# Pooled attention and a routed expert layer: VectorE's score differences first, banks by longest free, preparation at other steps

## The chip, the core and the metric

The program runs on one core of a Trainium2 chip. The metric is the device time of one execution in microseconds (us). A core has TensorE (PE; its weight loads are listed apart as PEld), VectorE (DVE), ScalarE (ACT), GpSimd (POOL) and SyncE (SP), which here issues the transfers between HBM and the on-chip memory SBUF. TensorE writes its results to PSUM, a small memory of banks that VectorE and ScalarE read. Each engine runs its instructions in order.

## What is computed

```python
# q, k, v: 8 batches, 8 heads, 1152 rows, 64 columns
q_pool = q.reshape(B, H, S // 2, 2, D).mean(axis=3)          # 576 pooled queries
scores = scale * np.matmul(q_pool, k.transpose(0, 1, 3, 2))
scores = scores - np.max(scores, axis=-1, keepdims=True)
attn = np.exp(scores)
attn = attn / (np.sum(attn, axis=-1, keepdims=True) + 1e-09)
x = np.matmul(attn, v)                                        # to 4608 tokens x 512
# expert layer: 8 experts, 512 -> 1024 -> 512
logits = x @ w_gate
e_idx = np.argmax(logits, axis=1)                             # one expert per token
gate_w = softmax(logits)[token, e_idx]
eom = 1.0 / (1.0 + np.exp(-(x @ w_output_gate)))
out = gate_w * eom[e_idx] * (np.maximum(x @ w1[e_idx], 0.0) @ w2[e_idx])
```

## The kernel before

Values are kept as a high and a low part (for instance `xk` and `kp` of k, `ph` and `pl` of the exponentials), and products are sums of two or three matmuls, so that the result has nearly 32-bit precision.

**Order.** Attention works on 32 pairs of heads (8 batches, 4 pairs each). A pair takes 18 steps: two heads, nine key blocks of 128 each. The main loop goes over the steps s of all pairs and writes out by hand the order of the instructions of TensorE, VectorE, ScalarE and GpSimd. The order of SP's transfers, and the place of the expert stage's first weight splits, are left to a planner that goes by its own costs. In the prediction "phase p" is step p of a pair. A step of the kernel before does, in this order:

1. `pendv`: the pending differences of the step before (below).
2. `pop()`: one entry of the list `fill` of small VectorE operations.
3. `scores` (L288, L290): four matmuls into one of two score buffers `sps`; then ScalarE takes the exponential twice. In twelve of the 18 steps GpSimd forms the low part `pl` (L304). In the six of `PLP` = 1, 3, 7, 9, 13, 15 (nine in the last pair) ScalarE writes the second exponential back to the score buffer (L294, L295), and VectorE forms `pl` from it (L298, the function `lo`), queued in `pendv` for the next step.
4. the row maxima that a later pair needs, one or two chunks: a group of matmuls L241 into a bank `mp`, and a VectorE maximum over it (L242), with a `pop()` after each. They run up to 18 steps ahead. After 15 and 27 chunks `rows` transposes the maxima on TensorE (L268) into a bank, and VectorE splits them into a high and a low part (L271, L272), which SP copies into rows 66 and 67 of `qb`.
5. P times V (`av`, L317 to L319) for the pair's probabilities, in bursts six or more steps later. After a head's ninth block two entries go to the head of `fill`: `e01` (L326, L327: the reciprocal of the row sum) and `e2` (L330: the scaling of the output into `xb`).
6. `routers`: the gate logits of a finished pair (`logits`: transposes L374, copies L378 on ScalarE, differences L381, matmuls L389, L393 on VectorE), every other step, at the end of odd steps; with a batch's last pair, `router` goes on with some 20 small VectorE operations (L418 to L478), a few per step, and five scatters on GpSimd. The router of the sixth batch is followed by `setup`, which picks the expert that comes first (L651 to L659 and on).

At three places within a step, `prep_at` issues the preparation of pairs to come, by the table `PREP`: each entry has a time in thirds of a step. `lk`, `lv` load q, k, v; `kh`, `qh` (ScalarE) and `kl`, `qsum`, `ql`, `qd` (GpSimd) split them; `dk`, `dq`, `dl` copy the parts on SP's queue; `amax` (ScalarE, L180) takes absolute sums of V; `gmax` (TensorE, L184) sums them over the partitions; `scale` turns this into a power of two on VectorE, GpSimd and VectorE; `vh` (ScalarE), `vs` and `vl` (GpSimd) scale and split V.

**Banks.** The chunk maxima, the transposes, the logits, `gmax` and the router share three PSUM banks. `psum()` hands them out in rotation and skips the ones in the set `ring[1]`, which only the router's two long-lived tiles enter. A new tile in a bank waits for the readers of the bank's previous tile.

After the attention, the expert stage gathers tokens in tiles of 256 and runs the two layers of their expert.

Of the kernel before, what the change touches and what calls it, by code (L numbers as in the profile page):

```python
# [8 lines left out]
F32 = mybir.dt.float32  # L9
# [6 lines left out]
ALU = mybir.AluOpType  # L16
# [4 lines left out]
L0 = 15.5  # L21
LS = 0.037
RI = 7
PREP = ((0, 'lk'), (12, 'kh', 0), (13, 'kh', 1), (12, 'qsum'), (15, 'kl'), (18, 'dk', 0), (19, 'dk', 1), (21, 'qh'), (26, 'ql'), (26, 'dq', 0), (27, 'dq', 1), (29, 'qd'), (32, 'dl', 0), (33, 'dl', 1),
        (53, 'lv'), (71, 'amax', 0), (74, 'amax', 1), (81, 'gmax'), (82, 'scale', 0), (85, 'scale', 1), (90, 'scale', 2), (93, 'vh', 0), (93, 'vs', 0), (96, 'vh', 1), (97, 'vl', 0), (100, 'vs', 1), (104, 'vl', 1))
BURST = {0: 2, 2: 2, 4: 2, 6: 2, 8: 1, 10: 2, 12: 2, 14: 2, 16: 3}
PLP = (1, 3, 7, 9, 13, 15)
PLPL = (1, 3, 5, 7, 9, 11, 13, 15, 17)
# [31 lines left out]
def attention(tc, qT, kT, vL, wg, keep, xrows, idscr, cum, pairs, setup, scat, init):  # L60
    nc = tc.nc
    nb = len(pairs) // 4
    with ExitStack() as ctx:
# [14 lines left out]
        ring = [0, set()]  # L78

        def psum(hold=False, name="tp"):  # L80

            ring[0] = next(i % 3 for i in range(ring[0] + 1, ring[0] + 4) if i % 3 not in ring[1])
            if hold:
                ring[1].add(ring[0])
            x = ps_m.tile([128, 512], F32, name=name, tag=f"mp{ring[0]}")
            return (x, ring[0]) if hold else x

        ident = keep['ident']
        onesf = keep['onesf']
# [22 lines left out]
        def prep(n, table):  # L112
# [67 lines left out]
                nc.scalar.activation(out=j, in_=vp[:, NC * h:NC * h + NC], func=AF.Abs, scale=2.0 ** -17, accum_out=am[:, h:h + 1])  # L180

            def gmax():
                g = psum()[:, 0:2]
                nc.tensor.matmul(g, lhsT=onesf, rhs=am, start=True, stop=True)  # L184
                gm.append(g)

            def scale(i):
                if i == 0:
                    nc.vector.tensor_scalar(out=ex, in0=gm[0].bitcast(U32), scalar1=0x7F800000, scalar2=None, op0=ALU.bitwise_and)
                elif i == 1:  # L190
# [69 lines left out]
                k -= 1  # L260

        pend_t = []

        def rows(force=False):
            while pend_t and (force or now[0] >= pend_t[0][-1] + TLAG):
                m9, nt, t0, t1, qbf, _ = pend_t.pop(0)
                tp = psum()[0:nt, 0:128]
                nc.tensor.transpose(out=tp, in_=m9[:, 0:nt], identity=ident)  # L268
                mr = sm.tile([5, 2, 128], F32R, name="mr")[0:nt]
                c0 = 16.0 * SHIFT  # L270
                nc.vector.tensor_scalar(out=mr[:, 0], in0=tp, scalar1=c0, scalar2=None, op0=ALU.subtract)  # L271
                nc.vector.scalar_tensor_tensor(out=mr[:, 1], in0=tp, scalar=c0, in1=mr.bitcast(F32)[:, 0], op0=ALU.subtract, op1=ALU.subtract)  # L272
                for j in range(2):
                    dmaf(qbf[66 + j:67 + j, 128 * t0:128 * t1].rearrange("o (t n) -> o t n", n=128), mr[:, j])

        pendv = []

        def scores(st, h):
            ka, kb, qa, qb = st['ka'], st['kb'], st['qa'], st['qb']
# [27 lines left out]
        def av(st, h, xb):  # L307
            vt = st['vt']
            a = ps_a.tile([128, 512], F32, name=f"av{st['n']}", tag="av")
            av_ = a[:, 0:325].rearrange("p (b x) -> p b x", x=65)  # L310
            pop(99)
            for c in range(NC):
                ph, pl = st['ph', h, c], st['pl', h, c]
                for qb in range(5):
                    q0 = 128 * qb if qb < 4 else NQ - 128
                    hi, lo = ph[:, q0:q0 + 128], pl[:, q0:q0 + 128]
                    nc.tensor.matmul(av_[:, qb, 0:65], lhsT=hi, rhs=vt[:, h, c, 0:65], start=c == 0 and qb == 0, stop=False)  # L317
                    nc.tensor.matmul(av_[:, qb, 0:64], lhsT=hi, rhs=vt[:, h, c, 66:130], start=False, stop=False)  # L318
                    nc.tensor.matmul(av_[:, qb, 0:65], lhsT=lo, rhs=vt[:, h, c, 0:65], start=False, stop=c == NC - 1 and qb == 4)  # L319
# [5 lines left out]
            def e01():  # L325
# [3 lines left out]
            def e2():  # L329
# [35 lines left out]
        def logits(b, c, xb):  # L365
# [2 lines left out]
            xl = sm.tile([128, NQ], F32R, name="xl", bufs=1)  # L368
            yield 1
            for c0, c1, grp in ((0, 256, (0, 1)), (256, NQ, (2, 3, 4))):  # L370
                tx = psum()
                for i, t in enumerate(grp):
                    x = xb[:, t, 128 * c:128 * c + 128]
                    nc.tensor.transpose(out=tx[:, 128 * i:128 * i + 128], in_=x, identity=ident)  # L374
                d = 0
                for o, w in ((0, c1 - c0),) if c0 == 0 else ((0, 256), (320, 64)):
                    z = slice(c0 + d, c0 + d + w)
                    nc.scalar.copy(out=xh[:, z], in_=tx[:, o:o + w])  # L378

                    def sub(o=o, w=w, z=z, tx=tx):  # L380
                        nc.vector.tensor_tensor(out=xl[:, z], in0=tx[:, o:o + w], in1=xh.bitcast(F32)[:, z], op=ALU.subtract)  # L381
                    fill.insert(0, sub)
                    d += w
                yield 1
# [15 lines left out]
        def router(b, xb):  # L400
# [40 lines left out]
            ring[1].discard(tk)  # L441
            yield 1
            rk, rkk = psum(True)
            rv = cut(rk, 0, 5, 8)
# [31 lines left out]
            cs = cut(rk, 96, 8)  # L476
            V.tensor_reduce(out=cs, in_=ohb.rearrange("p t e -> p e t"), axis=AX.X, op=ALU.add)
            V.tensor_tensor(out=cum, in0=cs, in1=cum, op=ALU.add)  # L478
            ring[1].discard(rkk)
            for t in range(5):  # L480
                for _ in range(3):
                    yield
# [6 lines left out]
                if t == 2 and b < nb - 1:  # L489
                    wr()  # L490
            if b == max(nb - 3, 0):
                yield from setup(psum)

        def sgen():
            for n in range(len(pairs)):
# [24 lines left out]
        def prep_at(s, ph):  # L520
            u = 3 * (s + SLEAD) + ph
            for n in range(max(u // 54 - 2, 0), min(u // 54 + 2, NP)):
                r = u - 54 * n + min(3 * (LEAD - 15), 2 * n)
                if r == 0:
                    preps[n] = prep(n, PREP)
                if n in preps:
                    for f in preps[n].pop(r, ()):
                        f()

        E = mybir.EngineType  # L530
        with tc.manual_schedule(engines={E.PE, E.DVE, E.Activation, E.Pool}):
# [15 lines left out]
            for s in range(18 * NP + 14):  # L547
# [52 lines left out]
class Moe:  # L600
# [35 lines left out]
    def setup(self, psum):  # L636

        nc, kp, k, P1 = self.tc.nc, self.kp, self.keep, self.P1
        V = nc.vector
# [5 lines left out]
        V.tensor_copy(out=cb, in_=self.cum)  # L645
        yield
        yield 1
        cp = psum()
        nc.tensor.matmul(cp[:, 0:8], lhsT=k['ones'], rhs=cb, start=True, stop=True)
        cn = kp.tile([128, 8], F32, name="cn1")  # L650
        V.tensor_copy(out=cn, in_=cp[:, 0:8])  # L651
        yield
        mx = kp.tile([128, 1], F32, name="mx1")
        em = k['em8'][:, 0]
        V.tensor_reduce(out=mx, in_=cn, axis=AX.X, op=ALU.max)
        V.tensor_tensor(out=cn, in0=cn, in1=mx.broadcast_to([128, 8]), op=ALU.is_equal)
        yield
        V.tensor_tensor(out=cn, in0=cn, in1=em, op=ALU.mult)
        V.tensor_reduce(out=mx, in_=cn, axis=AX.X, op=ALU.min)  # L659
        yield  # L660
        V.tensor_scalar(out=k['ef'][:, 1:2], in0=mx, scalar1=8.0, scalar2=None, op0=ALU.add)
        V.tensor_tensor(out=k['oh1'], in0=em, in1=mx.broadcast_to([128, 8]), op=ALU.is_equal)
        V.memset(k['ef'][:, 0:1], 0.0)
        yield
        V.tensor_copy(out=k['es'], in_=k['ef'][:, 1:2])
        ri = kp.tile([128, 2], U32, name="ri1")
        rb = kp.tile([128, 1], F32, name="rb1")
        V.tensor_scalar(out=rb, in0=k['ef'][:, 1:2], scalar1=float(ESTRIDE), scalar2=None, op0=ALU.mult)
        V.tensor_tensor(out=ri, in0=k['Tp'][:, 0], in1=rb.broadcast_to([128, 2]), op=ALU.add)
        yield  # L670
        self.gather_ids(-1, ri, kp, 1)
        for _ in range(8):
# [325 lines left out]
```

## Time and profile before

| | |
|---|---|
| median of 3 runs | 1615.24 us (1612.62 to 1616.14) |
| the profiled execution | 1615.64 us, span 1613.5 us |
| busy: PE, PEld | 1531.1 us (95%), 1415.6 us (88%) |
| busy: DVE, ACT, POOL | 1083.9, 1077.8, 997.9 us |
| granted TensorE clock, mean | 0.986 |
| attention, first to last score matmul | 34 to 1066 us |

In a row of a timeline the columns are start and duration in us, engine, line, operation, the tiles written and read, shapes, and how many equal instructions the row joins; in brackets stands how long the engine was idle before and what ended it. In a row of waits the columns are who waited for whom, us in total, times, and the longest. Matmuls are pipelined: a row's duration is its latency, and the distance of two starts is what one costs. Weight loads overlap the matmuls before them.

### The profile page before, as it was taken

The page shows a single profiled execution, that of the slowest core. Times are in us where ns is not written, and L with a number is a line of the kernel's source. Part 1 is how long each engine was busy: PE and PEld are TensorE (multiplying, and loading weights), DVE is VectorE, ACT ScalarE, POOL GpSimd, SP SyncE. Part 2 cuts the span into 40 slices and gives each one's busy share as a digit, 9 for nine tenths or more (in the row PEclk, how much of TensorE's full clock was granted, in tenths as well). Part 3 has the DMA queues.
Part 4 walks back from the last instruction along what each step waited for, and adds up shares of the span by engine and source line. Part 5 has one row for each costly group of instructions (what it writes and reads, how often), then busy time and mean ns, then how long its engine had stood idle before and what let it go on. Part 6 is the DMA issues. An engine that isn't in the chain of part 4 may idle for free. (4 is left out here: it accounts for less than half of the span.)

```text
span 1613.5 us, 42264 instructions
## 1 busy us (share of the span) xinstructions
PE 1531.1 (95%) x16618; PEld 1415.6 (88%) x16618; DVE 1083.9 (67%) x2222; ACT 1077.8 (67%) x1862; POOL 997.9 (62%) x917
## 2 busy tenths in 40 slices
PE   4999999999999999999999999979999999999997
PEld 4998989989989989988998898868999999999996
DVE  4676776777677677776777777656666666656663
ACT  2887878877878888888878787754445444544441
POOL 4887888788879788879788878634332232233200
PEclk9999999999999999999999999979999999999999
DMA  7765455655556467547655565256455645363500
GB/s 207 219 156 145 132 155 144 161 141 142 152 153 157 126 150 188 135 116 183 152 141 142 150 162 132 74 183 224 157 176 178 204 166 197 105 217 112 203 22 25
DMA packets 88755, 245.49 MB, mean 152 GB/s; under 512 B 13082, under 2 KB 17370, under 8 KB 88546
## 3 DMA queue, kind: packets, MB, share of 16 engines
q1 hardware_dynamic: 78826, 221.07, 49.1%
q0 software_dynamic: 9728, 21.67, 4.3%
q8 instruction: 135, 2.21, 0.6%
q14 instruction: 66, 0.54, 0.1%
HBM read 165.04 MB, written 23.81 MB: 117 GB/s over the span
## 5 line engine op out<-in xcount | busy, mean ns | idle before, releaser
L242 DVE TENSOR_REDUCE pm<-mp 128x1 f32<-128x384 f32 x864 | 457.6, 551 | 232.0 <-PE mp L241 226.3
L304 POOL TENSOR_TENSOR pl<-p,ph 128x576 f16<-128x576 f32 x381 | 489.3, 1286 | 182.1 <-ACT ph L303 146.0
L241 PE MATMUL mp<-ka,qa 128*128 128x384 f32 x960 | 319.7, 349 | 21.0 <-DMA qa<-yq 18.6
L302 ACT ACTIVATE p<-sps 128x576 f32<-128x576 f32 x381 | 250.8, 658 | 115.3 <-PE sps L290 108.4
L288 PE MATMUL sps<-qa,ka 128*128 128x288 f32 x1152 | 280.3, 325 | 24.1 <-DVE pl L298 17.8
L317 PEld LDWEIGHTS <-ph 128*128 128x128 f16 x2880 | 261.8, 97 | 42.2 <-issue 29.5
L317 PE MATMUL av<-vt,ph 128*128 128x65 f16 x2880 | 295.7, 194 | 0.0
L318 PE MATMUL av<-vt,ph 128*128 128x64 f16 x2880 | 293.3, 194 | 0.0
L319 PE MATMUL av<-vt,pl 128*128 128x65 f16 x2880 | 292.4, 192 | 0.0
L318 PEld LDWEIGHTS <-ph 128*128 128x128 f16 x2880 | 265.4, 97 | 0.4
L319 PEld LDWEIGHTS <-pl 128*128 128x128 f16 x2880 | 265.7, 99 | 0.0
L241 PE MATMUL mp<-kb,qb 66*128 66x384 f32 x768 | 263.4, 343 | 0.6 <-DMA kb<-kp 0.6
L290 PE MATMUL sps<-qb,kb 68*128 68x288 f32 x1152 | 248.8, 298 | 2.0 <-DMA qb<-mr 2.0
L303 ACT ACTIVATE ph<-sps 128x576 f16<-128x576 f32 x381 | 249.4, 655 | 0.0
L288 PEld LDWEIGHTS sps<-qa,ka 128*128 128x128 f32 x1152 | 184.3, 192 | 36.6 <-PE av L319 22.3
L241 PEld LDWEIGHTS mp<-ka,qa 128*128 128x128 f32 x960 | 181.3, 193 | 24.3 <-issue 20.6
L772 PE MATMUL hps<-xh,w1h 128*128 128x256 f32 x704 | 200.4, 285 | 0.0
L772 PE MATMUL hps<-xl,w1h 128*128 128x256 f32 x704 | 200.2, 284 | 0.0
L775 ACT ACTIVATE hh<-hps 128x512 fp32r<-128x512 f32 x88 | 52.6, 597 | 221.0 <-PE hps L772 221.0
L772 PE MATMUL hps<-xh,w1l 128*128 128x256 f32 x704 | 199.5, 283 | 0.0
L290 PEld LDWEIGHTS sps<-qb,kb 68*128 68x128 f32 x1152 | 187.4, 191 | 2.3 <-DMA qb<-mr 2.3
L294 ACT ACTIVATE ph<-sps 128x576 f16<-128x576 f32 x195 | 128.4, 658 | 84.2 <-PE sps L290 83.0
(170 smaller groups left out, 3191.4 us busy)
## 6 DMA issues: line engine op xcount, KB each, us to landing
ka<-xk SPq DMA_DIRECT2D x128, 288.0 KB
raw1b<-in_w_dram SPq DMA_DIRECT2D x24, 1024.0 KB
raw2b<-in_w_dram SPq DMA_DIRECT2D x24, 1024.0 KB
raw1a<-in_w_dram SPq DMA_DIRECT2D x22, 1024.0 KB
raw2a<-in_w_dram SPq DMA_DIRECT2D x22, 1024.0 KB
qp<-in_qT_dram SPq DMA_DIRECT2D x32, 576.0 KB
kpf<-in_kT_dram SPq DMA_DIRECT2D x32, 576.0 KB
vp<-in_vL_dram SPq DMA_DIRECT2D x32, 576.0 KB
```

The costliest lines, as they stand in the source:

```text
L241: nc.tensor.matmul(mp, lhsT=l, rhs=r, start=j == 0, stop=j == len(ops) - 1)
L242: nc.vector.tensor_reduce(out=pm[:, i:i + 1], in_=mp, axis=AX.X, op=ALU.max)
L288: nc.tensor.matmul(sps[:, j, 0:288], lhsT=ka[:, h, ks], rhs=qa[:, o + 288 * j:o + 288 * j + 288], start=True, stop=False)
L290: nc.tensor.matmul(sps[:, j, 0:288], lhsT=kb[:, h, ks], rhs=qb[:, h, 288 * j:288 * j + 288], start=False, stop=True)
L294: nc.scalar.activation(out=ph2, in_=x, func=AF.Exp, scale=1.0 / 16)
L302: nc.scalar.activation(out=p32.rearrange("p (j n) -> p j n", j=2), in_=x, func=AF.Exp, scale=1.0 / 16)
L303: nc.scalar.activation(out=ph2, in_=x, func=AF.Exp, scale=1.0 / 16)
L304: nc.gpsimd.tensor_tensor(out=pl, in0=p32, in1=ph, op=ALU.subtract)
L317: nc.tensor.matmul(av_[:, qb, 0:65], lhsT=hi, rhs=vt[:, h, c, 0:65], start=c == 0 and qb == 0, stop=False)
L318: nc.tensor.matmul(av_[:, qb, 0:64], lhsT=hi, rhs=vt[:, h, c, 66:130], start=False, stop=False)
L319: nc.tensor.matmul(av_[:, qb, 0:65], lhsT=lo, rhs=vt[:, h, c, 0:65], start=False, stop=c == NC - 1 and qb == 4)
L772: nc.tensor.matmul(hp[:, f], lhsT=W1[w][:, c, fs], rhs=d[x][:, c], start=i == 0, stop=i == 11)
```

## The change

- The table: a second one, `PREP`, serves the pairs from the third on; the old one, now `PREP0`, serves the first two. One `kh` goes from phase 5 to 6, `kl` from 6 to 7, `lv` from 0 to 4, the two `amax` from 6 and 7 to 10 and 12, `gmax` from 10 to 13, `scale` from 10, 11, 13 to 14, 14, 16, and the `vh`, `vs`, `vl` from phases 14 to 17 to phases 16 to 1 of the next pair.
- Banks: `psum()` gives the bank that has been free longest and that no tile holds. The transposed maxima, `gmax`'s sum, the logits' transposes and `setup`'s tile now hold their bank until their last reader is written out; `free` puts the bank at the end of the list.
- The split of the transposed maxima (`split`) goes into `pendv` and so to the start of the next step, behind `lo`. It does so from step 18 on.
- The routers' part of a step moves from the end of odd steps to the start of even ones, behind `pendv`.
- `e01` and `e2` become one entry, `norm`.
- `setup` keeps its counts in the PSUM bank instead of copying them to SBUF first, so its small operations read or write PSUM.

```diff
+PREP = ((0, 'lk'), (12, 'kh', 0), (12, 'qsum'), (17, 'kh', 1), (18, 'kl'), (18, 'dk', 0), (19, 'dk', 1), (22, 'qh'), (24, 'dq', 0), (25, 'dq', 1), (26, 'ql'), (29, 'qd'), (30, 'dl', 0), (32, 'dl', 1),
+        (63, 'lv'), (82, 'amax', 0), (88, 'amax', 1), (91, 'gmax'), (93, 'scale', 0), (94, 'scale', 1), (99, 'scale', 2), (100, 'vh', 0), (101, 'vs', 0), (103, 'vl', 0), (107, 'vh', 1), (107, 'vs', 1), (110, 'vl', 1))
...
-            ring[0] = next(i % 3 for i in range(ring[0] + 1, ring[0] + 4) if i % 3 not in ring[1])
+            while len(held) == 3:
+                pop() if fill else pendv.pop(0)()
+            k = next(i for i in banks if i not in held)
+            free(k)
             if hold:
-                ring[1].add(ring[0])
+                held.add(k)
...
+        def free(k):
+            held.discard(k)
+            banks.remove(k)
+            banks.append(k)
...
-                tp = psum()[0:nt, 0:128]
+                tp, tk = psum(True)
+                tp = tp[0:nt, 0:128]
                 nc.tensor.transpose(out=tp, in_=m9[:, 0:nt], identity=ident)
...
+                def split(tp=tp, tk=tk, mr=mr, qbf=qbf, t0=t0, t1=t1):
+                    nc.vector.tensor_scalar(out=mr[:, 0], in0=tp, scalar1=c0, scalar2=None, op0=ALU.subtract)
+                    nc.vector.scalar_tensor_tensor(out=mr[:, 1], in0=tp, scalar=c0, in1=mr.bitcast(F32)[:, 0], op0=ALU.subtract, op1=ALU.subtract)
+                    free(tk)
+                    for j in range(2):
+                        dmaf(qbf[66 + j:67 + j, 128 * t0:128 * t1].rearrange("o (t n) -> o t n", n=128), mr[:, j])
+                if now[0] < 18:
+                    split()
+                else:
+                    pendv.append(split)
...
-            fill[0:0] = [e01, e2]
+            fill.insert(0, norm)
...
-                tx = psum()
+                tx, tk = psum(True)
...
-        V.tensor_tensor(out=cn, in0=cn, in1=mx.broadcast_to([128, 8]), op=ALU.is_equal)
+        V.tensor_copy(out=ms, in_=mx)
+        V.tensor_tensor(out=eq, in0=cn, in1=ms.broadcast_to([128, 8]), op=ALU.is_equal)
...
                 while pendv:
                     pendv.pop(0)()
+                for r in routers:
+                    if not s % 2 or not live or not r[1]:
+                        r[1] = next(r[0], 0)
                 pop()
...
                 if not live:
                     pop(3)
-                for r in routers:
-                    if s % 2 or not live or not r[1]:
-                        r[1] = next(r[0], 0)
```

More of the change, by code (lines that the diff above doesn't have):

```diff
@@ L77, in attention @@
         ps_m = pool("ps_m", 1, space=PSUM)
-        ring = [0, set()]
+        banks, held = [0, 1, 2], set()
         def psum(hold=False, name="tp"):
-            ring[0] = next(i % 3 for i in range(ring[0] + 1, ring[0] + 4) if i % 3 not in ring[1])
+            while len(held) == 3:
+                pop() if fill else pendv.pop(0)()
+            k = next(i for i in banks if i not in held)
+            free(k)
             if hold:
-                ring[1].add(ring[0])
-            x = ps_m.tile([128, 512], F32, name=name, tag=f"mp{ring[0]}")
-            return (x, ring[0]) if hold else x
+                held.add(k)
+            x = ps_m.tile([128, 512], F32, name=name, tag=f"mp{k}")
+            return (x, k) if hold else x
+        def free(k):
+            held.discard(k)
+            banks.remove(k)
+            banks.append(k)
         ident = keep['ident']
@@ L182, in gmax @@
             def gmax():
-                g = psum()[:, 0:2]
+                g, gk = psum(True)
+                g = g[:, 0:2]
                 nc.tensor.matmul(g, lhsT=onesf, rhs=am, start=True, stop=True)
-                gm.append(g)
+                gm.extend((g, gk))
             def scale(i):
@@ L189, in scale @@
                     nc.vector.tensor_scalar(out=ex, in0=gm[0].bitcast(U32), scalar1=0x7F800000, scalar2=None, op0=ALU.bitwise_and)
+                    free(gm[1])
                 elif i == 1:
@@ L262, in attention @@
         pend_t = []
+        pendv = []
         def rows(force=False):
@@ L270, in rows @@
                 c0 = 16.0 * SHIFT
[L271 to L276, printed above, removed]
+                def split(tp=tp, tk=tk, mr=mr, qbf=qbf, t0=t0, t1=t1):
[8 more added lines that the diff above has]
+                    pendv.append(split)
         def scores(st, h):
@@ L323, in av, with norm @@
             H = 2 * st['p'][1] + h
-            def e01():
+            def norm():
                 nc.vector.tensor_scalar(out=r, in0=av_[:, :, 64], scalar1=1e-9 * math.exp(SHIFT), scalar2=st['sc'][:, h:h + 1], op0=ALU.add, op1=ALU.mult)
                 nc.vector.reciprocal(out=r, in_=r)
-            def e2():
                 nc.vector.tensor_tensor(out=xb[:, :, 64 * H:64 * H + 64], in0=av_[:, :, 0:64], in1=r.unsqueeze(2).broadcast_to([128, 5, 64]), op=ALU.mult)
@@ L378, in logits, with sub @@
                     nc.scalar.copy(out=xh[:, z], in_=tx[:, o:o + w])
-                    def sub(o=o, w=w, z=z, tx=tx):
+                    def sub(o=o, w=w, z=z, tx=tx, tk=tk if not d else None):
                         nc.vector.tensor_tensor(out=xl[:, z], in0=tx[:, o:o + w], in1=xh.bitcast(F32)[:, z], op=ALU.subtract)
+                        if tk is not None:
+                            free(tk)
                     fill.insert(0, sub)
@@ L440, in router @@
             V.tensor_tensor(out=so, in0=og, in1=ohb, op=ALU.mult)
-            ring[1].discard(tk)
+            free(tk)
             yield 1
@@ L478, in router @@
             V.tensor_tensor(out=cum, in0=cs, in1=cum, op=ALU.add)
-            ring[1].discard(rkk)
+            free(rkk)
             for t in range(5):
@@ L491, in router @@
             if b == max(nb - 3, 0):
-                yield from setup(psum)
+                yield from setup(psum, free)
         def sgen():
@@ L524, in prep_at @@
                 if r == 0:
-                    preps[n] = prep(n, PREP)
+                    preps[n] = prep(n, PREP if n > 1 else PREP0)
                 if n in preps:
@@ L634, in gather, with setup @@
             self.T[t]['xg'].append(xg)
-    def setup(self, psum):
+    def setup(self, psum, free):
         nc, kp, k, P1 = self.tc.nc, self.kp, self.keep, self.P1
@@ L647, in setup @@
         yield 1
-        cp = psum()
+        cp, ck = psum(True)
         nc.tensor.matmul(cp[:, 0:8], lhsT=k['ones'], rhs=cb, start=True, stop=True)
-        cn = kp.tile([128, 8], F32, name="cn1")
-        V.tensor_copy(out=cn, in_=cp[:, 0:8])
+        em = k['em8'][:, 0]
+        cn, eq, mx, mi = cp[:, 0:8], cp[:, 8:16], cp[:, 16:17], cp[:, 17:18]
+        V.tensor_reduce(out=mx, in_=cn, axis=AX.X, op=ALU.max)
         yield
[L653 to L656, printed above, removed]
+        ms = kp.tile([128, 1], F32, name="mx1")
+        V.tensor_copy(out=ms, in_=mx)
+        V.tensor_tensor(out=eq, in0=cn, in1=ms.broadcast_to([128, 8]), op=ALU.is_equal)
         yield
-        V.tensor_tensor(out=cn, in0=cn, in1=em, op=ALU.mult)
-        V.tensor_reduce(out=mx, in_=cn, axis=AX.X, op=ALU.min)
+        V.tensor_tensor(out=eq, in0=eq, in1=em, op=ALU.mult)
+        V.tensor_reduce(out=mi, in_=eq, axis=AX.X, op=ALU.min)
         yield
-        V.tensor_scalar(out=k['ef'][:, 1:2], in0=mx, scalar1=8.0, scalar2=None, op0=ALU.add)
-        V.tensor_tensor(out=k['oh1'], in0=em, in1=mx.broadcast_to([128, 8]), op=ALU.is_equal)
+        V.tensor_scalar(out=k['ef'][:, 1:2], in0=mi, scalar1=8.0, scalar2=None, op0=ALU.add)
+        V.tensor_tensor(out=k['oh1'], in0=em, in1=mi.broadcast_to([128, 8]), op=ALU.is_equal)
         V.memset(k['ef'][:, 0:1], 0.0)
         yield
-        V.tensor_copy(out=k['es'], in_=k['ef'][:, 1:2])
+        V.tensor_scalar(out=k['es'], in0=mi, scalar1=8.0, scalar2=None, op0=ALU.add)
         ri = kp.tile([128, 2], U32, name="ri1")
-        rb = kp.tile([128, 1], F32, name="rb1")
-        V.tensor_scalar(out=rb, in0=k['ef'][:, 1:2], scalar1=float(ESTRIDE), scalar2=None, op0=ALU.mult)
+        rb = cp[:, 18:19]
+        V.tensor_scalar(out=rb, in0=mi, scalar1=8.0, scalar2=float(ESTRIDE), op0=ALU.add, op1=ALU.mult)
         V.tensor_tensor(out=ri, in0=k['Tp'][:, 0], in1=rb.broadcast_to([128, 2]), op=ALU.add)
+        free(ck)
         yield
```

2 lines of the change are left out of this document (1 added, 1 removed).

## The prediction

> **What bounds the kernel now.** I read the page first (span and shares), then busy time in stretches, the waits of TensorE and of its weight loads, and the timelines of single steps. A pair of heads takes 18 steps; "phase p" is the p-th step of a pair, begun by the score matmuls at L288.
>
> ```profile
> span 1613.5 us, 42264 instructions
> 391.41:422.91 31.50, 30.81 (x414) 28.87 (x412) 22.35 (x53) 25.82 (x49) 25.16 (x23) 1.00 0.56 143
> 454.86:488.21 33.35, 31.33 (x420) 28.92 (x419) 24.37 (x69) 26.30 (x51) 26.95 (x25) 1.00 0.58 145
> ```
>
> The columns are us, then busy time of PE, PEld, DVE, ACT and POOL. The first stretch is an ordinary pair, the second one that also holds a batch's router. TensorE is busy for all but 0.69 us of the one and 2.02 us of the other; VectorE and ScalarE have slack. So TensorE bounds the attention, and the change can only remove what makes it wait. The expert stage is not edited. The waits of TensorE, then of its weight loads, from 130 to 1037 us (pairs 3 to 30; us, times, longest):
>
> ```profile
> PE sps L288 <- DVE pl L298: 12.7, 44, 0.5
> PE tp L374 <- DVE cum L478: 7.7, 7, 1.1
> PE mp L241 <- DVE xl L381: 2.0, 1, 2.0
> PEld sps L288 <- PE av L319: 21.0, 65, 0.6
> PEld sps L288 <- issue: 4.2, 21, 0.2
> ```
>
> Most waits are those of score matmuls. Scores use two buffers, so step s+1 waits for all readers of step s-1; in six steps of a pair the last reader is VectorE's difference "lo" (L298). The loads show 86 such waits, of which 44 are also idle time of the array.
>
> **A. lo ahead of the other VectorE work.** Phase 15 of an ordinary pair; the last two rows are an unhindered start:
>
> ```profile
> 416.19 0.65 ACT L295 ACTIVATE sps<-sps 128x576 f32<-128x576 f32 x1
> 416.48 0.55 DVE L242 TENSOR_REDUCE pm<-mp 128x1 f32<-128x384 f32 x1
> 416.95 0.47 DVE L393 TENSOR_TENSOR lT<-tp,lT 32x320 f32<-32x320 f32 x1
> 417.34 0.73 DVE L298 TENSOR_TENSOR pl<-sps,ph 128x576 f16<-128x576 f32 x1
> 417.78 0.19 PE L319 MATMUL av<-vt,pl 128*128 128x65 f16 x1
> 418.22 0.37 PE L288 MATMUL sps<-qa,ka 128*128 128x288 f32 x1 [0.25 <-DVE pl L298]
> ...
> 411.26 0.19 PE L319 MATMUL av<-vt,pl 128*128 128x65 f16 x1
> 411.29 0.50 PE L288 MATMUL sps<-qa,ka 128*128 128x288 f32 x2
> ```
>
> Stalled, L288 starts 0.44 us after the last P V matmul, unhindered 0.03: the stall costs 0.41 us, its idle time of 0.25 plus 0.16 for the weights that could not be loaded ahead. lo's data were ready at 416.84 (L295's end), yet lo began at 417.34, behind the router's L393. With lo first it begins at about 416.95, 0.39 us earlier, more than the idle 0.25. Phases 3 and 17 have the same form: at 3 the transposed maxima stand in front (L271 here, L272 after it), at 17 L330.
>
> ```profile
> 426.07 0.65 ACT L295 ACTIVATE sps<-sps 128x576 f32<-128x576 f32 x1
> 426.82 0.27 DVE L271 TENSOR_SCALAR mr<-tp 4x128 fp32r<-4x128 f32 x1
> 427.33 0.73 DVE L298 TENSOR_TENSOR pl<-sps,ph 128x576 f16<-128x576 f32 x1
> 428.21 0.50 PE L288 MATMUL sps<-qa,ka 128*128 128x288 f32 x2
> 420.71 0.75 DVE L298 TENSOR_TENSOR pl<-sps,ph 128x576 f16<-128x576 f32 x1
> ```
>
> At 3, lo moves from 427.33 to 426.82, 0.51 earlier. At 17 the closing operations now run in one block before the maxima; lo (420.71) keeps its work in front, but the next item lets the PE arrive later, so I count only part of it. Moving the split of the maxima one step later also delays two small DMAs of qb (SP's queue) by at most a step; the rows they feed are used five steps later or more. The router's and the closing operations keep their TensorE order.
>
> **B. ScalarE's preparation spaced.** Phase 9 is another case: VectorE is idle before lo.
>
> ```profile
> 404.40 0.70 ACT L180 ACTIVATE junk<-vp 128x576 f16<-128x576 f32 x1
> 405.06 0.67 ACT L294 ACTIVATE ph<-sps 128x576 f16<-128x576 f32 x1
> 405.59 0.68 ACT L295 ACTIVATE sps<-sps 128x576 f32<-128x576 f32 x1
> 406.37 0.76 DVE L298 TENSOR_TENSOR pl<-sps,ph 128x576 f16<-128x576 f32 x1 [0.83 <-POOL pl L304]
> 407.28 0.50 PE L288 MATMUL sps<-qa,ka 128*128 128x288 f32 x2 [0.24 <-DVE pl L298]
> ```
>
> lo starts 0.10 after L295's end (406.27), so ScalarE ends it, whatever the view names; L180 (the absolute maximum of V) runs right ahead of L294. The new table takes L180 out of phases 6 and 7 (to 10 and 12) and one k cast from 5 to 6. L180 and the read of its sum hold ScalarE from 404.40 to 405.06, so L294 can go up to 0.66 us earlier: the idle 0.24 goes. The V operations on GpSimd come later in its queue, by one to two steps; their readers are four steps away. SP's V load, which waits for the last of them, also issues later, but the first use of that load moves by more (from phase 6 to 10).
>
> Price of A and B: the 44 waits average 12.7/44 = 0.29 us idle, plus 0.16, is 0.45 each: 19.8 us. The other 42 (65+21-44) have little idle time; at 0.16 to 0.3 each, taken as 0.22, 9.2 us. Together 29 us. I take 28, leaving 1 for phase 17. From below, nothing goes if ScalarE sets lo everywhere; from above, 31.
>
> **C. Banks by longest free.** In a router pair the logits' transposes (L374) took the bank the router had just released:
>
> ```profile
> 457.67 0.34 PE L241 MATMUL mp<-ka,qa 128*128 128x384 f32 x1
> 457.84 0.33 PE L241 MATMUL mp<-kb,qb 66*128 66x384 f32 x1
> 457.87 1.02 DVE L242 TENSOR_REDUCE pm<-mp 128x1 f32<-128x384 f32 x2 [0.94 <-PE mp L241]
> 458.48 0.27 PE L268 MATMUL tp<-ident,m 128*4 128x128 f32 x1 [0.30 <-DVE pm L242]
> ...
> 468.64 0.34 PE L241 MATMUL mp<-kb,qb 66*128 66x384 f32 x1
> 470.09 0.44 PE L374 MATMUL tp<-ident,xb 128*128 128x128 f32 x2 [1.11 <-DVE cum L478]
> ```
>
> L374 starts 1.45 after the matmul before it. I wrote out the order in which banks are handed out: under the new rule it gets the bank of the first of the two maxima just before it. That is exactly what L268 does in the same pair already, and L268 starts 0.64 after its predecessor. So the wait shrinks by 1.45 - 0.64 = 0.81 us and does not vanish: 7 x 0.81 = 6 us. L268's own stall stays.
>
> The same listing shows one place that gets worse, in every pair. At phase 14 the second logits matmul (L389) gets the bank of the first of phase 13's two maxima, since the preparation's small matmul (L184) now sits in phase 13 and holds a bank.
>
> ```profile
> 441.35 0.28 PE L184 MATMUL tp<-am,onesf 128*128 128x2 f32 x2
> 441.49 0.42 PE L241 MATMUL mp<-ka,qa 128*128 128x384 f32 x1
> 447.17 0.65 ACT L294 ACTIVATE ph<-sps 128x576 f16<-128x576 f32 x1 [0.79 <-PE sps L290]
> 447.52 1.02 DVE L242 TENSOR_REDUCE pm<-mp 128x1 f32<-128x384 f32 x2 [0.73 <-PE mp L241]
> 447.67 0.31 PE L389 MATMUL tp<-xh,wgt 128*128 128x320 f32 x1
> ```
>
> The first of those two reductions ends about half-way, 448.07 (one takes 0.55, as at 416.48). L268 starts 0.06 after the reduction that it waits for (457.87 + 0.55 to 458.48); so L389 can start at 448.13. It would be there at 447.67 plus 0.14 for L184 (441.35 to 441.49), 447.81: a new stall of 0.32 us in some 28 pairs, 9 us. Its ends are 0, if VectorE comes earlier than now, and 0.47 (L268's 0.64 less the 0.17 between two L241 starts), 13 us. It also delays the arrival at phase 15, where lo then is no longer late.
>
> **D. The set-up operations, and one early pair.**
>
> ```profile
> 890.75 3.38 DVE L656 TENSOR_TENSOR cn<-cn,mx 128x8 f32<-128x8 f32 x1
> 151.00:154.40 3.40, 3.27 (x39) 2.96 (x40) 0.70 (x3) 0.42 (x1) 1.46 (x3) 0.69 1.02 222
> 895.00:899.00 4.00, 3.92 (x42) 3.72 (x42) 2.85 (x13) 1.07 (x2) 0.76 (x3) 0.68 1.03 226
> ```
>
> L656, 128x8 values, occupies VectorE for 3.38 us; TensorE stands still behind it for about 2 us, then runs at a granted clock of 0.68 for 4 us (1.3 us lost). The change gives it a PSUM operand, as in the router's small operations. It also holds a bank through the set-up, which I price at up to three stalls like L268's (0.47 each): net 2 us. In pair 3 the wait of L241 on L381 (2.0) and the clock of 0.69 after it (3.4 x 0.31 = 1.1) come from a bank that the new rule does not hand out: 3 us. These two stalls stay below the idle window of about 3.4 us after which the clock halves by the Trainium skill ("TensorE: Matmul & The Clock Gate", Part 1). By that rule the two items would bring 2.4 us less, 1588 us in all; the rows show the lower clock, and I go by them.
>
> **Edits priced at nothing.** `norm`: the same three VectorE operations, now together at the start of phases 5 and 15; they end before the maxima of that step are due at 0.47 distance (416.48 to 416.95), and their reader, the next P V burst, is a step away. If that cover is gone, one P V burst waits some 0.4 us per head. The k cast, `kl` and the q parts keep their order on GpSimd and their copies still leave SP's queue several steps before the maxima read them; a copy that came late would stop TensorE at L241, which the waits above show for no copy. The first two pairs keep the old table.
>
> Sum: -28 - 6 + 9 - 2 - 3 = -30. From the profiled execution, 1615.64 us (its span of 1613.5 and 2.1 around it; 0.4 above the median of 1615.24), that gives 1585.6; against the median, 1585. The placement of the experts' first weight splits between the last pair's operations is left to the planner; I bound that by +-4 us.
>
> **The rivals.** (1) Smaller gain: the bank wait at phase 14 costs its upper 13 us, and phase 17 and a third of phase 15 keep their stalls because VectorE's work is only reordered (another 11 us): 1600. For it: VectorE keeps every operation. Against it: it is busy 22 of 31.5 us. (2) Larger gain: no stall at phase 14: 1576. For it: VectorE idles 0.73 us before the first of the reductions; against it: that idle time is a wait for the matmul itself. (3) No change: ScalarE, not the queue order, ends every lo; A and B's 28 us stay and 1613 comes out. Phase 9 speaks for it, the rows of phases 3 and 15 against. (4) Slower: the sum matrix multiplication L184 at phase 13 now follows its input, the second L180 at phase 12, by one step instead of two. If ScalarE finishes that late, TensorE, in order, waits in each pair. L180 takes 0.9 us and fits the 0.79 idle ahead of L294 (447.17) nearly; from about 1.1 us of wait per pair (30 us over 28 pairs) the change loses, and at 1.5 us it gives 1585 + 42 = 1627. Nothing in the trace shows ScalarE that late in this phase.
>
> **How the numbers follow.** Forecast 1585 (its own range 1577 to 1593) 0.52; smaller gain 0.21; larger gain 0.14; no change 0.05; slower 0.08. Runs of this kernel spread by 0.2%, about what can be told from no change. The first three are faster: 0.87; no change 0.05; slower 0.08. The range leaves out the last two and the tails of (1) and (2): 1568 to 1606.
>
> **What would show it.** Waits of L288 on L298 fall from 44 to a handful; those of L374 on L478 vanish and some 0.3 us on L242 take their place; a new wait of L389 on L242 appears in every pair; ordinary pairs take about 30.5 us instead of 31.5, router pairs 31.8 instead of 33.35; L656's successor takes 0.2 us. It would be wrong if L288 still waits as often, if L184 waits for ScalarE, or if the new bank waits are longer than L268's.

## The result and the profile after

The changed kernel takes 1598.1 us (median; 1596.47 to 1605.6), the kernel before 1615.69 (1612.62 to 1616.83): a ratio of 0.990 (95% interval 0.987 to 0.993). It is faster by 17.6 us where 30 were forecast: inside the range, 13 above the forecast. The profiled execution is the longest of the four, 1605.6 us, 7.5 above the median. So what is counted in its trace below is probably more than a median execution lost.

Line numbers are those of the changed kernel: scores L307 and L309 (before L288, L290), maxima's matmul and reduction L253 and L254 (L241, L242), transposed maxima L282 and their split L287, L288 (L268, L271, L272), lo L317 (L298), P V L336 to L338 (L317 to L319), closing operations L345 to L347, the logits' transposes and matmuls L391 and L408 (L374, L389), the preparation's sum L195 (L184), its reader L200 (L189).

The page's head, and TensorE's waits between 130 and 1037 us (line, what is waited for; us, times, longest):

```profile
span 1603.8 us, 42290 instructions
```

```profile
PE sps L309 <- DMA qb<-mr: 8.9, 6, 2.6
PE tp L391 <- DVE pm L254: 2.4, 8, 0.3
PE tp L282 <- DVE pm L254: 2.1, 7, 0.3
PE mp L253 <- DVE lT L412: 1.0, 2, 0.8
PE sps L307 <- DVE pl L317: 0.8, 2, 0.6
```

and of its weight loads in the same window:

```profile
PEld tp L408 <- DVE pm L254: 11.2, 28, 0.6
```

Of the 44 waits of scores on lo, 2 are left. In their place stands a line that the kernel before did not have: the second score matmul, L309, waits for a DMA that brings the split maxima into qb. The weight loads show the forecast wait of the logits' second matmul, 28 times. Three pairs in a row, with the granted clock as the third number from the end:

```profile
358.70:389.30 30.60, 30.52 (x414) 28.66 (x413) 22.40 (x53) 26.27 (x49) 28.35 (x26) 1.00 0.60 154
389.30:424.85 35.55, 33.63 (x415) 31.33 (x413) 22.53 (x53) 26.26 (x49) 25.11 (x23) 0.90 0.55 142
424.85:456.00 31.15, 31.09 (x419) 28.93 (x419) 23.14 (x57) 26.24 (x49) 25.39 (x25) 1.00 0.56 145
```

Pair 10 is what the prediction describes, 30.6 us and TensorE busy for all but 0.08. Pair 11 does the same work in 35.5, at a clock of 0.90. Its beginning:

```profile
389.32 0.43 PE L307 MATMUL sps<-qa,ka 128*128 128x288 f32 x2
391.60 0.82 PE L309 MATMUL sps<-qb,kb 68*128 68x288 f32 x2 [1.85 <-DMA qb<-mr]
```

and the 12 us that follow, in stretches of 4:

```profile
391.60:395.60 4.00, 4.00 (x38) 3.69 (x39) 0.56 (x1) 1.86 (x3) 2.85 (x3) 0.50 0.04 16
395.60:399.60 4.00, 4.00 (x45) 3.64 (x44) 2.71 (x6) 2.38 (x4) 1.42 (x2) 0.69 0.37 101
399.60:403.60 4.00, 4.00 (x64) 3.85 (x64) 2.56 (x6) 2.37 (x4) 2.20 (x2) 1.00 0.14 51
```

Unhindered, L309 follows L307 by 0.27 us; here by 2.28, so the wait itself costs 2.01. Then the clock is 0.50 for 4 us and 0.69 for the next 4: 4 x 0.50 + 4 x 0.31 = 3.2 us more. Together that is 5.2, about pair 11's excess of 5.0.

Why the DMA is late stands in SP's queue during pair 10 (start, us; the issues of one pair, then those of the same pair before):

```profile
374.35 0.33 SPq L144 DMA_DIRECT2D qp<-in_qT_dram  x1
374.78 3.96 SPq L120 DMA_DIRECT2D ka<-xk  x4
...
385.05 0.46 SPq L120 DMA_DIRECT2D kb<-kp  x1
385.75 1.57 SPq L120 DMA_DIRECT2D qb<-mr  x2
```

```profile
372.86 0.33 SPq L134 DMA_DIRECT2D qp<-in_qT_dram  x1
373.29 3.83 SPq L110 DMA_DIRECT2D ka<-xk  x4
...
384.19 1.58 SPq L110 DMA_DIRECT2D qb<-mr  x2
```

Twelve copies go out one after another behind q's load, 374.78 to 385.5, and the two of mr stand behind them. Their data had long been there: the split of the maxima ended at 381.50, 4.25 us before its copies left.

```profile
381.22 0.28 DVE L288 SCALAR_TENSOR_TENSOR mr<-tp,mr 5x128 fp32r<-5x128 f32 x1
```

Before and after, the split ends 7.8 us ahead of the next pair. The load of q opens the series: it overwrites the one q tile, so it waits until GpSimd's sum of q (L158) has read it, and the copies wait behind it in the queue. SP's longest wait in this stretch, then GpSimd's rows in the same pair, and before:

```profile
SPq L144 <- POOL yq L158: 5.8, 1, 5.8
```

```profile
370.63 0.99 POOL L502 DMA_INDIRECT idscr<-tid,posi  x1 [0.17 <-PE av L338]
371.65 1.31 POOL L323 TENSOR_TENSOR pl<-p,ph 128x576 f16<-128x576 f32 x1
372.89 1.43 POOL L158 TENSOR_TENSOR yq<-qp 128x576 f32<-128x576 f32 x1
```

```profile
371.39 1.44 POOL L148 TENSOR_TENSOR yq<-qp 128x576 f32<-128x576 f32 x1
```

The sum ends at 374.32, 15.6 us after the pair's start (358.73); before, at 372.83, 13.75 after 359.08. It is so in all five pairs in which the router's scatters run too (6, 10, 14, 18 and 22): the sum ends 1.8 us later, and pair 10 has become 1.7 us shorter. mr now leaves 3.6 us ahead of its pair (385.75 to 389.32); before, 7.2 (384.19 to 391.38).

### The profile page after: what moved, and what is told of

Same layout as the page of the kernel before. It is cut to its first block, busy times and chain, and to the rows that moved or that the text cites. A ratio compares the mean times of both kernels' runs of the same rounds, so it can differ in the third digit from the quotient of the medians.

```text
span 1603.8 us, 42290 instructions
## 1 busy us (share of the span) xinstructions
PE 1531.7 (96%) x16618; PEld 1413.5 (88%) x16618; DVE 1082.6 (68%) x2222; ACT 1086.7 (68%) x1862; POOL 994.6 (62%) x917
## 5 line engine op out<-in xcount | busy, mean ns | idle before, releaser
L254 DVE TENSOR_REDUCE pm<-mp 128x1 f32<-128x384 f32 x864 | 456.8, 551 | 254.3 <-PE mp L253 248.9
L253 PE MATMUL mp<-ka,qa 128*128 128x384 f32 x960 | 319.2, 349 | 20.6 <-DMA qa<-yq 18.6
L336 PEld LDWEIGHTS <-ph 128*128 128x128 f16 x2880 | 263.8, 97 | 42.9 <-issue 33.2
L336 PE MATMUL av<-vt,ph 128*128 128x65 f16 x2880 | 299.0, 195 | 0.0
L338 PE MATMUL av<-vt,pl 128*128 128x65 f16 x2880 | 295.6, 193 | 0.0
L307 PE MATMUL sps<-qa,ka 128*128 128x288 f32 x1152 | 282.7, 327 | 6.4 <-DVE pl L317 6.3
L338 PEld LDWEIGHTS <-pl 128*128 128x128 f16 x2880 | 267.5, 99 | 0.0
L309 PE MATMUL sps<-qb,kb 68*128 68x288 f32 x1152 | 251.7, 301 | 14.8 <-DMA qb<-mr 14.8
L253 PE MATMUL mp<-kb,qb 66*128 66x384 f32 x768 | 264.3, 344 | 0.6 <-DMA kb<-kp 0.6
L309 PEld LDWEIGHTS sps<-qb,kb 68*128 68x128 f32 x1152 | 189.3, 193 | 16.5 <-DMA qb<-mr 16.5
L253 PEld LDWEIGHTS mp<-ka,qa 128*128 128x128 f32 x960 | 182.0, 194 | 23.5 <-issue 18.9
L307 PEld LDWEIGHTS sps<-qa,ka 128*128 128x128 f32 x1152 | 185.6, 193 | 10.4 <-DVE pl L317 7.0
```

The source lines that it names most:

```text
L253: nc.tensor.matmul(mp, lhsT=l, rhs=r, start=j == 0, stop=j == len(ops) - 1)
L254: nc.vector.tensor_reduce(out=pm[:, i:i + 1], in_=mp, axis=AX.X, op=ALU.max)
L307: nc.tensor.matmul(sps[:, j, 0:288], lhsT=ka[:, h, ks], rhs=qa[:, o + 288 * j:o + 288 * j + 288], start=True, stop=False)
L309: nc.tensor.matmul(sps[:, j, 0:288], lhsT=kb[:, h, ks], rhs=qb[:, h, 288 * j:288 * j + 288], start=False, stop=True)
```

## The experiments

Times are medians. "Stall" is how much later than unhindered a TensorE instruction starts after its predecessor; sums of stalls are over pairs 2 to 30 of the profiled run.

**e1: the split of the maxima at once.** It asks whether mr is late because the split was put off.

```
-                if now[0] < 18:
+                if True:
                     split()
```

> The changed kernel, but the transposed maxima are split at once as before, not one step later. What is to be explained: in the changed kernel the score matmuls L309 wait for the copy qb<-mr in 6 pairs (8.9 us between 130 and 1030 us), and the time is 1598 where 1585 was forecast. Theory Q (queue): SP's queue is late, because its q load waits for GpSimd's sum of q (L158), which GpSimd reaches later since the V operations moved into the steps before it; the copy of the maxima stands behind. By Q the L309 waits stay (4 to 7 of them) and the phase 3 stalls of 0.25 us come back in some 20 pairs: 1600 to 1606. Rival S (split): the copy is late because the split itself moved one step back. By S the L309 waits vanish: 1586 to 1592.

1602.09 us, ratio 0.9925 (0.9907 to 0.9943). The waits on mr stay:

```profile
PE sps L309 <- DMA qb<-mr: 5.2, 5, 1.5
```

The deferral is not their cause. What it buys shows as well: phase 3's stalls return, 0.25 us in 20 pairs, 5.0 in all.

**e4: GpSimd's sum of q ahead of the k cast.**

```
-((0, 'lk'), (12, 'kh', 0), (12, 'qsum'), ...
+((0, 'lk'), (8, 'qsum'), (12, 'kh', 0), ...
```

> The changed kernel with one entry moved: GpSimd's sum of q (qsum) 4 thirds of a step earlier, ahead of one or two of GpSimd's differences pl. Theory Q: the sum ends 1.3 to 2.6 us earlier, SP's queue starts as much earlier, most L309 waits after pair 3 vanish: 1586 to 1592, with the phase 13 to 14 wait (0.23 us in 27 pairs) still there. Rivals S and K: nothing changes, 1598.

1591.94 us, ratio 0.9859 (0.9839 to 0.9878), against 0.9903 for the change: its waits on L309 vanish from pair 2 on. SP's queue in pair 10, which starts at 351.73 and ends at 382.33:

```profile
363.53 0.33 SPq L144 DMA_DIRECT2D qp<-in_qT_dram  x1
...
376.59 1.73 SPq L120 DMA_DIRECT2D qb<-mr  x2
```

mr leaves 5.7 us ahead of the next pair, and pair 11 takes 30.49 us instead of 35.53. That shows the cause of the waits behind the router's scatters: the load of q behind a late sum held back the copies, and these held back mr. In the changed kernel the pairs hit (7, 11, 15, 17, 19, 23) exceed their undisturbed neighbours by 1.6, 5.0, 1.6, 0.6, 5.9 and 3.3, 18 us in all. (Pair 17's 0.6 has another origin, since the sum ahead of it is not late.) Of the two profiled executions e4's is 14.3 us shorter, mainly by these 18 and by 6.8 in pair 1, less 9 in pairs 26 and 27; by the medians it is 6. Pair 26, which sets up the expert stage, went from 31.9 to 39.5 us:

```profile
856.80 4.45 DVE L664 COPY cb<-cum 128x8 bf16<-128x8 bf16 x1
...
857.31 1.31 POOL L323 TENSOR_TENSOR pl<-p,ph 128x576 f16<-128x576 f32 x1
858.55 1.44 POOL L158 TENSOR_TENSOR yq<-qp 128x576 f32<-128x576 f32 x1
859.93 1.28 POOL L323 TENSOR_TENSOR pl<-p,ph 128x576 f16<-128x576 f32 x1
```

The first row is VectorE, the others GpSimd beside it. A copy of 128x8 values (0.16 us in the changed kernel) holds VectorE until 861.25, just past the end of GpSimd's third operation in a row at 861.21. The same copy took 3.07 us in e1, 1.53 in e2, 1.86 in e3 and 2.99 in e10, and ended each time 0.04 us after an operation of GpSimd. Pair 26 takes 34.4 to 36.7 us in these four runs, so that 2 to 5 us of what separates them from the change lies there.

**e5: that copy on ScalarE, beside e4's edit.**

```
-        V.tensor_copy(out=cb, in_=self.cum)
+        nc.scalar.copy(out=cb, in_=self.cum)
```

> The sum of q ahead of the k cast, as in e4, and the set-up's cast of the counts (L664) on ScalarE instead of VectorE. Theory P: L664 took 4.45 us in e4 because it could not finish while GpSimd ran four operations back to back, and 0.16 us in the changed kernel where GpSimd was free beside it; on ScalarE it does not wait. Pair 26 goes from 39.48 to some 32.5 us and pair 27 from 31.9 to 30.5, so 1583 to 1585. Rival: the next small VectorE operation of the set-up waits in its place, or pair 26 is long for another reason: 1590 to 1593.

1588.43 us, ratio 0.9845 (0.9821 to 0.987). Pair 26 falls from 39.48 to 33.04 and the copy takes 0.2 us, as theory P said; the rival's next operation did not wait. The 3 us above the expectation are in pair 1, 37.0 instead of 32.5: there L309 waits 2.15 us in this run and 0.62 in e4's, though mr left 2.99 us ahead of the pair in both.

**e6: the preparation's sum L195 two places later, beside e5's edits.**

```
-(91, 'gmax'), (93, 'scale', 0), (94, 'scale', 1)
+(93, 'gmax'), (95, 'scale', 0), (96, 'scale', 1)
```

> As e5, and the preparation's sum L195 from phase 13 to phase 14 (93 instead of 91; its reader and the next step at 95 and 96). Theory: the new stall of L408 on the maxima at phase 14 (0.23 us in 27 pairs, 6.3 us) is only a matter of which bank comes free, and it vanishes: 6 us below e5, some 1577 to 1579. Rival: the later sum delays the scales, the cast of V follows late, and P V waits at the next pair's beginning; or the wait goes to another matmul: within 2 us of e5.

1580.76 us, ratio 0.9795 (0.9778 to 0.9813), 8 us below e5. The wait of L408 falls from 28 places to one, and ordinary pairs from 30.5 to 30.2 us:

```profile
PEld tp L408 <- DVE pm L254: 0.6, 1, 0.6
```

**e2 and e3: the table.** e2 takes back the V part alone, e3 the whole table.

```
e2 -(63, 'lv'), (82, 'amax', 0), (88, 'amax', 1), (91, 'gmax'), ...
   +(53, 'lv'), (71, 'amax', 0), (74, 'amax', 1), (81, 'gmax'), ...
e3 -preps[n] = prep(n, PREP if n > 1 else PREP0)
   +preps[n] = prep(n, PREP0)
```

> The changed kernel with the old times for V (lv, amax, gmax, scale, vh, vs, vl), the new ones for q and k kept. Theory Q: the sum of q ends at most 14.3 us after the start of its pair instead of up to 15.6, the L309 waits vanish (13 us gained), the new phase 13 to 14 wait of L408 vanishes too since gmax is back in phase 10 (6 us gained), and the phase 9 stalls of 0.4 us come back in up to 18 pairs (7 us lost) or less, because the k cast stays moved: 1585 to 1590. Rival S: the L309 waits stay, about 1598. Rival K (the later k cast and kl delay SP's copies ka<-xk): the L309 waits stay as well.

> The changed kernel with the old table for all pairs: the order on VectorE and the banks are new, the preparation is not spaced. Theory Q: no L309 waits, no phase 13 to 14 wait, phase 9 stalls back (18 x 0.4 = 7 us): 1588 to 1593. Rival K: here, and not with the old V times alone, the L309 waits vanish. Rival S: L309 waits stay, about 1600.

e2: 1610.67 us, 0.9971 (0.996 to 0.9983). e3: 1606.09, 0.9947 (0.993 to 0.9964). In both the waits on mr are gone after pair 1, as e4's explanation wants (GpSimd's V work is early again), yet both are slower than the change. Pair 1 itself keeps its wait in e2 (37.4 us) and loses it in e3 (32.0). Waits of e2, then of e3:

```profile
PE sps L307 <- DVE pl L317: 11.6, 24, 1.0
PE sps L307 <- ACT ph L322: 4.9, 6, 1.5
```

```profile
PE sps L307 <- ACT ph L322: 9.3, 6, 2.2
PE sps L307 <- DVE pl L317: 5.4, 18, 0.6
```

Phase 9's stalls are back (12.3 us in e2, 8.1 in e3), and at phase 8 a new one of 0.7 to 2.4 us appears in the pairs after a router, where scores wait for ScalarE. I had expected 1585 to 1593, 13 to 26 us less. Some 5 us of it is pair 26; also without these, what the V part of the table takes from ScalarE's way is worth more than what it loses on SP.

**e7, e9, e10: the corners of table and banks.** e7 is the kernel before with the new table alone; e9 the kernel before with the bank rule alone (and banks held until read); e10 the changed kernel with the old order of VectorE's work, so table, banks and the new set-up without the order.

```
e7  +preps[n] = prep(n, PREP if n > 1 else PREP0)
e9  +k = next(i for i in banks if i not in held); free(k)
e10 -for r in routers: ...        (ahead of pop())
    +for r in routers: ...        (at the step's end)
    +if True: split()
    +fill[0:0] = [e01, e2]
```

> The kernel before with the new table from pair 2 on and nothing else: order of VectorE's work, banks and set-up as before. If the parts add up (e3, without the table, 1606; the changed kernel 1598), the table is worth 8 us: 1607, with the waits of L309's namesake (L290) on the maxima's copies as in the changed kernel and the stalls of phase 9 gone. Rival: the table pays only where VectorE takes the differences first; then only the losses of SP's queue and the clock after them show: 1618 to 1628.

> The kernel before with banks by longest free (and held until read) and nothing else: old table, old order, old set-up. Theory 'add up': with the old table the bank of the sum L195 never stopped TensorE, so the rule is worth the two items that the prediction names, the logits' transposes in router pairs (6 us) and pair 3 (3 us): 1605 to 1609. Rival: it only pays together with the table (which alone cost 25 us): 1612 to 1617.

> The changed kernel with the order of VectorE's work as before (router's step at the end, split of the maxima at once, closing operations in two parts); table, banks and set-up as changed. With e7 (table alone, 1640.5), e9 (banks alone) and before it makes the four corners of table and banks. Theory: banks take back what the table alone costs and the pair of them gains without the order, the order brings the rest by the stalls at phases 3, 15 and 17 (0.25 to 0.41 us each in most pairs): 1604 to 1612. Rival: the order brings nothing measurable (1596 to 1600), or it is what makes the table pay (1615 or more).

| | ratio to before | interval |
|---|---|---|
| bank rule alone (e9, 1603.94 us) | 0.9946 | 0.9929 to 0.9964 |
| table alone (e7, 1640.53 us) | 1.0176 | 1.0145 to 1.0206 |
| both, old order (e10, 1606.25 us) | 0.9955 | 0.9938 to 0.9973 |
| bank rule, order and set-up, old table (e3) | 0.9947 | 0.993 to 0.9964 |
| the change | 0.9903 | 0.9874 to 0.9932 |

The table alone costs 27 us, against both theories, and after pair 1 the waits on mr that I expected in it do not come in its longer pairs. One wait is the largest part of it (e7's line numbers: L243 maxima, L191 the sum's reader):

```profile
PE mp L243 <- DVE ex L191: 20.2, 26, 0.9
```

```profile
357.98 0.73 DVE L300 TENSOR_TENSOR pl<-sps,ph 128x576 f16<-128x576 f32 x1
358.65 0.14 DVE L191 TENSOR_SCALAR ex<-tp 128x2 uint32<-128x2 uint32 x1
358.84 0.44 PE L243 MATMUL mp<-ka,qa 128*128 128x384 f32 x1 [0.77 <-DVE ex L191]
```

In the new table the sum sits at phase 13. With banks in turn its bank comes round at phase 14, while its reader L191 still stands behind lo on VectorE: 0.93 us in each of 27 pairs, 25 us. The logits' new stall at phase 14, pair 1 and pairs 26 and 27 cost 6 us each on top, and the stalls of phases 9 and 15 that the table removes give 20 back. The longest-free rule gives another bank. Bank rule and table are thus not additive: 0.9946 and 1.0176 would make 1.012, e10 has 0.9955. The bank rule alone brings 9 to 10 us, as theory 'add up' and the prediction's 6 + 3 had it, but that is in part luck: its trace has 5.6 us from the logits' transposes, 1.7 from pair 3, and 3.6 from pair 26, where the old set-up's comparison (the prediction's L656) happened to take 0.31 us and not 3.38. Beside the bank rule the table brings nothing measurable with the old order (e10 beside e9). The order of VectorE's work is worth some 8 us with the table (0.9955 to 0.9903, the size that e10's theory gave), 3.6 of them in pair 26, and nothing measurable without it (e3 beside e9, where pair 26 costs e3 4.6 us).

**e8: banks in turn in the changed kernel.**

```
-            k = next(i for i in banks if i not in held)
-            free(k)
+            k = next(i for i in (1, 2, 0, 1, 2)[last[0]:last[0] + 3] if i not in held)
+            last[0] = k
```

> The changed kernel with banks handed out in turn again (held ones skipped), everything else as changed. By the order in which the banks would be handed out, the stall of L408 at phase 14 stays (0.23 us in 27 pairs). Theory: longest free is worth what the prediction says of it: L391 waits again for the router's reduction, 1.45 instead of 0.6 to 0.8 us in seven pairs (6 us) and pair 3 loses 3 us: 1604 to 1608. Rival: with the router's work moved to the front of the step the bank is free in time whatever the rule: within 2 us of the changed kernel's 1598.

1635.77 us, ratio 1.0147 (1.0124 to 1.017): both theories are far off, since neither had the sum's bank in it. The same wait as in e7, and the logits' transposes behind the router's reduction, 2.0 instead of 1.1 us (L251 maxima, L198 the reader, L389 transposes):

```profile
PE mp L251 <- DVE ex L198: 17.1, 27, 1.3
PE tp L389 <- DVE cum L495: 13.8, 7, 2.0
```

**e11 and e12: two parts of the order, on e6.** e11 sets the closing operations in two parts again (`fill[0:0] = [e01, e2]`); e12 puts the router's step back to the step's end, as in e10's first two lines.

> As e6 (1580.8), with the closing operations of P V in two parts again. Theory: they run beside other work either way, and only the logits start later by the distance of the second part: within 3 us of 1580.8. Rival: the second part falls behind lo or the maxima again at phases 5, 15 and 17, 0.3 us or more in most pairs: 1588 to 1600.

> As e6 (1580.8), with the logits' and the router's step at the end of a step again, so that its VectorE work stands ahead of lo. Theory: lo is late at phase 15 behind L412 (0.41 us in 28 pairs, 11 us) and, where the router's other items fall on odd phases, at two or three more in seven pairs (3 to 8 us): 1592 to 1600. Rival: lo's place is now set by ScalarE alone, within 3 us of 1580.8.

e11: 1580.36 us, 0.9799 (0.9775 to 0.9823), no difference from e6. Its stalls at phase 17 are 0.27 us in 22 pairs, 5.8 us; e6 has 4.9, in the router pairs and pair 26. e12: 1575.78 us, 0.9775 (0.9749 to 0.9802), the fastest kernel seen, though the interval overlaps e6's. Neither theory had it more than 3 us faster. lo is late at phase 15 again, but by 0.20 us in each pair and not 0.41. In ordinary pairs half of that is given back ahead of phase 17, and they are 0.1 longer than e6's. Router pairs are 0.3 to 0.7 shorter, since e6, where the router's work runs at the front, has 0.4 to 0.8 of stall at their phase 17. Pair lengths (us, from one L307 at phase 0 to the next):

```
pair      6      7      8      9(router) 10     11     12     26+27
before    31.52  31.47  31.97  33.35     32.30  31.53  31.95  67.20
after     30.45  32.02  31.11  31.86     30.59  35.53  31.13  62.42
e4        30.49  30.49  31.12  32.01     30.60  30.49  31.13  71.38
e6        30.23  30.20  30.76  31.95     30.23  30.26  30.78  64.87
e12       30.33  30.34  30.93  31.69     30.31  30.35  30.93  62.10
```

e12's ordinary pairs 10 and 11 and the first of its next batch:

```profile
350.99:381.30 30.31, 30.28 (x414) 28.68 (x413) 22.27 (x53) 26.19 (x49) 28.19 (x26) 1.00 0.59 151
381.30:411.64 30.34, 30.31 (x413) 28.68 (x413) 22.29 (x53) 26.22 (x49) 25.12 (x23) 1.00 0.55 148
411.64:442.58 30.94, 30.90 (x419) 29.02 (x418) 22.93 (x57) 26.23 (x49) 25.46 (x25) 1.00 0.55 146
```

## Why the prediction was right, and where it failed

**The step that failed** is "Edits priced at nothing": "their copies still leave SP's queue several steps before the maxima read them". They did; no L253 waits for a copy. But behind the copies stood mr, the other customer of that queue, and its reader is L309, in the first step of the next pair. I had asked of the split whether it delays mr (by at most a step, I wrote, and with five steps or more to spare; the split's end did not move, and it was 7.8 us, four and a half steps), and not of GpSimd's later V operations whether they delay the load at the head of the queue. Part B says that these operations "come later in its queue, by one to two steps", looks at their own readers, and stops there; what they push back, the sum of q, was the chain. It cost 18 us in pairs 7 to 23 of the profiled run. Pair 1 of that run is 7.9 us longer than before (39.38 against 31.51), also with a late mr, but not by this chain alone: pair 1 stays long with the old V times (37.4 in e2) and mostly with the early sum (37.0 in e5, 35.6 to 38.4 in e6, e11 and e12), and is 32.0 with the old table (e3). What in the table does it is open. Without these 26 us the profiled run would stand near 1580. The moved steps thus brought some 36 us where I had summed 30; so the range held in part by luck, because the terms that I had summed came out larger and stood against a loss that was not in the sum.

**A and B** (28 us): right, and a little small. The stalls of scores at phases 3, 9, 15 and 17 were 5.0, 7.5, 13.0 and 5.9 us before, 31.4 in all; none above 0.1 us is left there. Ordinary pairs take 30.5 us as forecast, with 0.23 us of new stall in them. At phase 15 the two parts overlap. I put its 0.41 us on VectorE's order, because L393 ran ahead of lo, and the order with the old table does leave nothing there in ordinary pairs (e3). But the table with the old order leaves only 0.13 (e10), and with the router's old place 0.20 (e12): ScalarE's spacing alone would have brought half of it or more. Phase 3 was the order, but at 0.25 us and not 0.45. The closing operations in one part remove the 0.27 us at phase 17 of ordinary pairs, which e11 has again, but on e6 that brought no time.

**C**: the logits' transposes, forecast to shrink by 0.81 us, go from a stall of 1.26 to 0.46 in seven pairs, 5.6 us for 6. The new stall of L408 exists in every pair and measures 0.23 instead of 0.32, 6.3 us instead of 9:

```profile
418.25 0.34 PE L253 MATMUL mp<-kb,qb 66*128 66x384 f32 x1
418.66 0.42 PE L408 MATMUL tp<-xh,wgt 128*128 128x320 f32 x1
```

0.41 us from start to start, against 0.17 between the maxima. The mechanism was right too: moving the sum (e6) takes it away. What my sum of the terms did not need, and I did not see, is that the old rule would have stopped the new table (e7).

**D**: pair 3 went from 34.4 to 31.74 (3 us forecast), pair 26 from 35.67 to 31.92, 3.8 us where I took 2. The comparison that took 3.38 us takes 0.17 with its PSUM operand, here and in every run with the new set-up. But pair 26's gain is in part luck: the set-up had one more operation of that kind, L664, which met only a scatter of GpSimd here and a row of operations in e4, where it cost more than L656 had; and e9, with the old set-up, has pair 26 at 32.1.

**The rivals.** The time came out at rival (1)'s 1600 by another way than its own; none of its three conditions occurred. Rival (4), L195 waiting for ScalarE, shows as one wait of 0.4 us in the whole stage. Rival (3), that ScalarE ends every lo, does not hold for phases 3 and 15: the order alone, with the old table, leaves no stall there in ordinary pairs (e3). Rival (2), no stall at phase 14, was not there in this kernel, and e6 made it.

## What to carry to other kernels

When a step moves to a later place on an engine, follow not only its own readers but what it pushes back on that engine, and from there into the queue that waits for it: here three links (GpSimd's V work, the sum of q, q's load at the head of SP's queue) lie between the edit and the DMA that TensorE waited for. Half of the slack that went from 7.2 to 3.6 us was lost to the later sum, the other half to the pair that had become shorter: faster work around a transfer uses up its slack. Test the parts of a change in pairs as well as alone: the table cost 27 us alone, brought nothing measurable with the bank rule, and paid only with the rule and the order (the change beside e3: 8 us, 4.8 of them in pair 26). And compare two runs pair by pair before a difference is put down to an edit: up to 5 us of several of these lie in one pair, 26, where a small copy met GpSimd or missed it.

## What the runs showed of the hardware

A wait of 1.85 us on TensorE (pair 11) was followed by 4 us at a granted clock of 0.50 and 4 more at 0.69, one of 2.58 (pair 19) by 0.50 and 0.67, one of 1.44 (pair 23) by 0.61 and 0.97; the two waits of about 2 us that the prediction quoted had shown 0.68 and 0.69. After 1.30 and 1.32 us (pairs 7 and 15) the clock stayed at 1.00, and in e1 it did after 1.51 (pair 19), so the length of the wait alone does not decide. By the Trainium skill ("TensorE: Matmul & The Clock Gate", Part 1: The HAM clock gate) the clock halves after at least one idle window of about 3.4 us, a window that runs freely; the trace shows the half clock that it states, but after shorter waits. The stall of 2.0 us in pair 11 cost 5.0; those of 1.5 in pairs 7 and 15 cost 1.6.

A VectorE copy of 128x8 values from SBUF to SBUF lasted 4.45 us while GpSimd ran one operation after another, and 0.16 us in the changed kernel; on ScalarE it took 0.2 in the same place. By the Trainium skill ("SBUF — State Buffer", "SBUF: two separate sides") VectorE's two-port modes and GpSimd share a port pair that is locked for a whole instruction. The trace agrees, and adds that VectorE did not get it between GpSimd's operations: it was held through three of them. That the copy ran in such a mode no run shows.
